# A channel DFT split into even and odd channels, with its sums spread over the product that follows

## The chip, the cores and the metric

The kernel runs on one core of a Trainium2 chip. The metric is the time of one execution in microseconds (us) on the device. Engines are named as in the profile: PE is TensorE's matrix multiply, PEld its weight load, DVE is VectorE, ACT is ScalarE, POOL is GpSimd, SP is SyncE, which here only issues transfers.

## What is computed

Rows of `x` (2048 tokens by 640 channels) are normalized; the result is the sum of `x`, a Fourier transform over channels and tokens of which the real part is kept, and a two-layer product over tokens.

```python
xn = layernorm(x)                                   # (1, 2048, 640)
a = einsum("bsd,ed->bse", xn, dft_hid_re)           # DFT over channels
b = einsum("bsd,ed->bse", xn, dft_hid_im)
y = einsum("ts,bse->bte", dft_seq_re, a) - einsum("ts,bse->bte", dft_seq_im, b)
u = gelu(einsum("bsd,sf->bdf", xn, w1) + b1)        # F = 1728
v = einsum("bdf,fs->bds", u, w2) + b2
out = x + y + v.transpose(0, 2, 1)
```

The kernel has a second way for DFT matrices without the symmetries that it uses; checks of those matrices, which run beside the products, decide at the end whether it is taken. It is not taken here.

## The kernel before

**Stages on TensorE, one after the other.** The first product (`up`, with `w1`); the token DFT (`seq_order`, from L619); the channel DFT (`hid_step`, L736); the second product (`down_step`, L837, with `w2`); then the last row tile is stored. Every float32 matmul is made of three (`three`, L135 to L140): an operand is cut into a high and a low part (`high` on ScalarE L130, `low` on VectorE L133), and high x high, high x low and low x high are accumulated in one bank of PSUM. There are eight banks, taken in turn by `bank()`.

**The channel DFT.** The token DFT leaves blocks T0 to T4 of folded channels: cosine rows of even channels (T0) and odd ones (T1), sine rows (T3, T4), and T2, which mixes what is left of both. The weights of a matmul are 128 tokens of such a block, the moving operand is a piece of the channel matrix with EW = 162 columns for one half of the outputs. Since output 320 - e differs from output e only in the sign of the odd channels, one piece serves both halves. Before, `hid_high` and `hid_low` (L681 to L697) lay each piece twice, the second time with the sign of the odd channels, and `hid_products` (L725) makes three products of 2 x 162 = 324 columns into one bank: T2, the even block, the odd block. The two halves of the bank then hold both halves of the outputs. `part` 0 is cosine, 1 is sine.

A step is one `products(s)` (L741): two groups (`part` 0 and 1), one bank each, for 128 tokens. `hid_step(n, odd, i)` has two steps, s = 0 and 1, and four banks; n runs over `order` (L807): (odd, i) = (1,0), (1,1), (0,0), (0,1). At n = N_MID a fifth bank takes two rows for the middle tokens, with weights of two columns (`t_mid_cut`). When both steps of an n are done, ScalarE copies two of the four banks (`copies`, L753) and VectorE makes sums and differences with the other two (`sums`, L758: four operations of 324); a row of outputs is joined by `whole_rows` (L712: four operations of 159 to 161) and stored to `y_dram`, plain by SP or mirrored by POOL's indirect transfer (`scatter`, L719); ScalarE turns each row round for the mirrored tokens (`read_back`, L775), and that is stored too. So an n makes four pieces of 128 x 640.

**The second product.** 16 row tiles of 128 tokens, each of four steps (i = 0 to 3): 24, 24, 24 and 10 matmuls of 320 columns, 82 in all. The first two tiles go by turns, so that all steps with i = 0 come first. A step's weights, a piece of `w2`, are cut two steps ahead (AHEAD = 2), into three buffers (`cut0` to `cut2`). For tile t, `rest_load` (L872) brings the rows of `y_dram` and of `x`, `rest_sum` (L877) adds them, `down_read` (L880) adds the two banks and `b2`, `store` (L890) writes the tile out.

**What sets the order.** A loop over all steps (L1259 to L1273) writes the instructions out: for step i first what stands in `loads` (SP), then the high part of step i + 2's piece on ScalarE, `reads` (in the token DFT behind the high part, elsewhere ahead), `middle`, the low part on VectorE, `measures`, `behind`, and last the matmuls of step i. `at(i, f)` puts f into such a list. Every engine runs its instructions in this order, and a waiting instruction holds those behind it on its engine; SP too, so a store that waits for its tile holds the loads behind it. s_hid and s_down are the first steps of the channel DFT and of the second product. A step of the second product is counted from s_down in what follows. The checks' 48 loads (`late`, from L1151, 40 by SP and 8 in two parts by POOL) are spread evenly from step `begin` to `n_steps - 9`, each compared five steps after its load.

Of the kernel before, what the change touches and what calls it, by code (L numbers as in the profile page):

```python
# [16 lines left out]
P = 128  # L17
# [32 lines left out]
def fnet_plus_mixer(  # L50
# [630 lines left out]
    def hid_high(q):  # L681
        if not hid_cut:
            hid_cut.append(keep.tile([P, 2, 4, 2, EW], R32, name="hid_main", tag="zt"))
            hid_cut.append(keep.tile([P, 2, 4, EW], R32, name="hid_mix", tag="ck0"))
        hid_main, hid_mix = hid_cut
        raw, by = hid_place[0], -1.0 if q > 1 else 1.0
        nc.scalar.activation(hid_main[:, 0, q, 0], raw[:, q], AF.Copy, scale=by)
        nc.scalar.activation(hid_mix[:, 0, q], raw[:, 4], AF.Identity, scale=mask[:, q : q + 1])

    def hid_low(q):  # L690
        hid_main, hid_mix = hid_cut
        raw, by = hid_place[0], -1.0 if q > 1 else 1.0
        for to, hi, of, times in (
            (hid_main[:, 1, q, 0], hid_main[:, 0, q, 0], q, by), (hid_mix[:, 1, q], hid_mix[:, 0, q], 4, mask[:, q : q + 1])
        ):
            nc.vector.scalar_tensor_tensor(to, raw[:, of], times, hi.bitcast(F32), op0=ALU.mult, op1=ALU.subtract)
        nc.scalar.activation(hid_main[:, :, q, 1], hid_main[:, :, q, 0].bitcast(F32), AF.Copy, scale=-1.0 if q % 2 else 1.0)  # L697
# [4 lines left out]
    def y_place(n):  # L702

        if n not in y_tiles:
            if n % 6 < 2:
                t = keep.tile([P, 2, 2 * D + 1], F32, name=f"y{n}", tag="n3")
                y_tiles[n - n % 2], y_tiles[n - n % 2 + 1] = t[:, 0], t[:, 1]
            else:
                y_tiles[n] = keep.tile([P, 2 * D + 1], F32, name=f"y{n}", tag=f"h{n - 2}")
        return y_tiles[n][:, : D + 1], y_tiles[n][:, D + 1 :]  # L710

    def whole_rows(y, a, b, e=EW):  # L712
        v = nc.vector
        v.tensor_add(y[:, : e4 + 1], a[:, : e4 + 1], b[:, : e4 + 1])
# [21 lines left out]
    def hid_step(n, odd, i):  # L736
# [16 lines left out]
        def copies():  # L753
            held.append(keep.tile([P, 4, 2 * EW], F32, name=f"sums{n}", tag=f"n{1 + n % 2}"))
# [29 lines left out]

        def read_mid():
            a, y = mid_bank[0], keep.tile([P, D], F32, name="y_mid", tag="ck1")[0:2]
            for to, of in (
                (y[:, : e4 + 1], a[:, : e4 + 1]), (y[:, 2 * e4 - 1 : e4 : -1], a[:, EW + 1 : EW + e4]),
                (y[:, 2 * e4 : 3 * e4 + 1], a[:, EW : EW + e4 + 1]), (y[:, D - 1 : 3 * e4 : -1], a[:, 1:e4]),
            ):  # L790
                nc.scalar.activation(to, of, AF.Copy)
# [6 lines left out]
        at(step + 2, copies, when=reads)  # L798
        at(step + 2, sums, when=reads)
        at(step + 2, read(0), when=reads)  # L800
        at(step + 3, read(1), when=reads)
        at(step + 3, read_back(0))
        at(step + 4, read_back(1))
        if n == N_MID:
            at(step + 2, read_mid, when=reads)

    order = [(odd, i) for odd in (1, 0) for i in range(NJ)]  # L807
# [6 lines left out]

    def h_high(i):
# [594 lines left out]
```

## Time and profile before

| | |
|---|---|
| time, median of 3 runs | 442.91 us (442.82 to 443.01) |
| profiled execution | 442.86 us, of which 441.1 is the span between its first and last instruction |
| mean granted clock of TensorE | 0.996 |
| channel DFT, first to last matmul start | 219.83 to 242.32 us |
| second product, first to last matmul start | 242.47 to 434.51 us |
| bytes moved | 105.69 MB |

A time in a row of the timeline is counted from the span's start. In the rows of groups, "x32 | 9.9, 310 | 0.0" is the count, the time in which the group was busy, the mean ns of one, and the idle time ahead. In the rows of waits stand who waited for what, the total in us, the count and the longest. In the rows of windows stand the stretch, its length, each engine's busy time (with the count of instructions), the clock, the busy share of the 16 DMA engines, and GB/s. Transfers of the second product, as the page lists them:

```profile
check<-in_dft_seq SPq DMA_DIRECT2D x58, 512.0 KB
...
w_raw<-in_w SPq DMA_DIRECT2D x16, 512.0 KB
w_raw<-in_w SPq DMA_DIRECT2D x16, 384.0 KB
rest<-y SPq DMA_DIRECT2D x16, 320.0 KB
rest<-in_x SPq DMA_DIRECT2D x16, 320.0 KB
out<-rest SPq DMA_DIRECT2D x15, 320.0 KB
```

### The profile page before, as it was taken

What the parts mean: (1) busy time and instruction counts of PE and PEld (TensorE: products, weight loads), DVE (VectorE), ACT (ScalarE), POOL (GpSimd) and SP (SyncE); (2) the same over time, 40 slices, a digit from 0 to 9 for tenths busy, and PEclk for the clock granted to TensorE, in tenths of its full rate; (3) what the DMA queues carried; (4) which work ended last, traced back from release to release, by engine and by line L of the source; (5) the groups of instructions that cost most, each with busy time, mean ns of one, the idle gap of its engine ahead of it and who ended that gap; (6) DMA issues with size and microseconds to landing.
All of it is one profiled execution on the core that took longest, in us unless ns stands there. A gap on an engine that the chain in (4) does not pass through costs nothing.

```text
span 441.1 us, 8064 instructions
## 1 busy us (share of the span) xinstructions
PE 433.1 (98%) x2963; PEld 427.5 (97%) x2963; DVE 320.4 (73%) x662; ACT 248.5 (56%) x477; POOL 76.7 (17%) x120
## 2 busy tenths in 40 slices
PE   8999999999999999999999999999999999999994
PEld 4999999999999999999999999999999999999993
DVE  6976644776967778777888659677877768688771
ACT  6866673676555655467755535536555455546540
POOL 2055511032220001100023320111302304101000
PEclk9999999999999999999999999999999999999998
DMA  8882508698884760413314999999998998979301
GB/s 291 303 293 83 178 2 292 217 336 291 259 296 161 237 193 25 121 49 97 121 59 192 317 409 403 395 364 357 334 375 309 330 381 292 395 265 347 143 31 39
DMA packets 48176, 105.69 MB, mean 240 GB/s; under 512 B 5732, under 2 KB 6644, under 8 KB 48128
## 3 DMA queue, kind: packets, MB, share of 16 engines
q1 hardware_dynamic: 44816, 93.50, 60.2%
q0 software_dynamic: 3168, 11.42, 7.3%
q8 instruction: 25, 0.41, 0.4%
q14 instruction: 23, 0.19, 0.1%
q10 hardware_dynamic: 144, 0.16, 0.1%
HBM read 94.58 MB, written 10.49 MB: 238 GB/s over the span
## 4 chain that ended last, share of the span: by engine, by line
PE 93%; DVE 3%; DMA 1%; ACT 1%; issue 0%; SPq 0%; DVEq 0%
PE psum L138 26%; PE psum L139 26%; PE psum L140 26%; PE psum L293 9%; PE psum L283 2%; PE psum L863 2%; DMA w_raw<-in_w 1%; DVE early L133 1%; DVE st L200 1%; DVE x L133 1%; ACT early L130 0%; DVE zt L247 0%; DVE r L230 0%; ACT zt L245 0%; DVE again L231 0%
## 5 line engine op out<-in xcount | busy, mean ns | idle before, releaser
L133 DVE TENSOR_TENSOR piece<-w_raw,piece 128x512 fp32r<-128x512 f32 (+2 forms) x128 | 76.4, 598 | 78.3 <-ACT piece L130 69.5
L138 PE MATMUL psum<-h_cut,piece 128*128 128x320 f32 x416 | 128.6, 309 | 0.0
L139 PE MATMUL psum<-h_cut,piece 128*128 128x320 f32 x416 | 128.4, 309 | 0.0
L140 PE MATMUL psum<-h_cut,piece 128*128 128x320 f32 x416 | 128.4, 309 | 0.0
L130 ACT ACTIVATE piece<-w_raw 128x512 fp32r<-128x512 f32 (+2 forms) x112 | 67.0, 600 | 108.5 <-PE psum L140 78.7
L138 PE MATMUL psum<-x,piece 128*128 128x320 f32 x288 | 89.0, 309 | 0.0
L140 PE MATMUL psum<-x,piece 128*128 128x320 f32 x288 | 88.9, 309 | 0.0
L139 PE MATMUL psum<-x,piece 128*128 128x320 f32 x288 | 88.8, 308 | 0.0
L985 ACT ACTIVATE check<-check 128x1024 f32<-128x1024 f32 (+2 forms) x66 | 65.1, 987 | 28.0 <-DVE check L968 11.4
L140 PEld LDWEIGHTS psum<-h_cut,piece 128*128 128x128 f32 x416 | 78.1, 188 | 0.0
L138 PEld LDWEIGHTS psum<-h_cut,piece 128*128 128x128 f32 x416 | 78.1, 188 | 0.0
L139 PEld LDWEIGHTS psum<-h_cut,piece 128*128 128x128 f32 x416 | 78.1, 188 | 0.0
L293 PE MATMUL psum<-x,early 128*128 128x320 f32 x384 | 57.6, 310 | 0.9 <-DVE early L133 0.3
L293 PEld LDWEIGHTS psum<-x,early 128*128 128x128 f32 x384 | 56.3, 188 | 2.1 <-ACT early L130 1.2
L140 PEld LDWEIGHTS psum<-x,piece 128*128 128x128 f32 x288 | 54.1, 188 | 0.0
L138 PEld LDWEIGHTS psum<-x,piece 128*128 128x128 f32 x288 | 54.1, 188 | 0.0
L139 PEld LDWEIGHTS psum<-x,piece 128*128 128x128 f32 x288 | 54.1, 188 | 0.0
L948 POOL DMA_INDIRECT check<-in_dft_seq,from_seq x16 | 19.5, 1221 | 115.7 <-ACT check L985 113.2
L133 DVE TENSOR_TENSOR x<-zt,x 128x640 fp32r<-128x640 f32 x16 | 13.1, 818 | 14.6 <-ACT x L130 14.6
L721 POOL DMA_INDIRECT y<-y,to_mirror x8 | 10.4, 1303 | 57.3 <-DVE y L717 52.7
L883 DVE SCALAR_TENSOR_TENSOR rest<-psum,b_sb,rest 128x320 f32<-128x320 f32 x32 | 16.1, 543 | 1.0 <-PE psum L863 1.0
L966 DVE TENSOR_TENSOR check<-check,check 128x512 f32<-128x512 f32 x24 | 15.4, 685 | 0.0
(215 smaller groups left out, 615.7 us busy)
## 6 DMA issues: line engine op xcount, KB each, us to landing
check<-in_dft_seq SPq DMA_DIRECT2D x58, 512.0 KB
w_raw<-in_w SPq DMA_DIRECT2D x56, 256.0 KB
w_raw<-in_w SPq DMA_DIRECT2D x16, 512.0 KB
w_raw<-in_w SPq DMA_DIRECT2D x16, 384.0 KB
rest<-y SPq DMA_DIRECT2D x16, 320.0 KB
rest<-in_x SPq DMA_DIRECT2D x16, 320.0 KB
out<-rest SPq DMA_DIRECT2D x15, 320.0 KB
ck<-in_dft_seq SPq DMA_DIRECT2D x6, 512.0 KB
```

The costliest lines, as they stand in the source:

```text
L130: nc.scalar.activation(hi, src, AF.Copy)
L133: nc.vector.tensor_sub(lo, src, hi.bitcast(F32))
L138: nc.tensor.matmul(bank, wh, mh, start=first, stop=False, skip_group_check=True)
L139: nc.tensor.matmul(bank, wh, ml, start=False, stop=False, skip_group_check=True)
L140: nc.tensor.matmul(bank, wl, mh, start=False, stop=last, skip_group_check=True)
L283: nc.tensor.matmul(to[half][:, :H2], w[0][:, c], m[i], start=k == to[2] and i == 0, stop=k == to[3] and i == 1, skip_group_check=True,)
L293: nc.tensor.matmul(up_banks[f][half][:, :H2], w_cut[f, k // G][part == 2][:, c], n[:, part == 1, k % 2, half * H2 : (half + 1) * H2], star ...
L721: nc.gpsimd.indirect_dma_start(to, bass.IndirectOffsetOnAxis(ap=to_mirror[:, j : j + 1], axis=0), y, None,)
L883: nc.vector.scalar_tensor_tensor(rest[t][:, 1, cols], down_banks[t][half][:, :H2], b2_sb[:, t : t + 1], rest[t][:, 0, cols], op0=ALU.add, ...
L948: nc.gpsimd.indirect_dma_start(to[:, c * CH : (c + 1) * CH], None, dft_seq.rearrange("c k p t -> (c k p) t"), bass.IndirectOffsetOnAxis(ap ...
L966: (v.tensor_add if odd != (i == 4 and m) else v.tensor_sub)(x1, x0, x1)
L985: nc.scalar.activation(v, v, AF.Square, accum_out=off[:, n : n + 1])
```

## The change

**Products.** The piece of the channel matrix is laid once, without signs. A group multiplies the even block into the first 162 columns of its bank, the odd block into the other 162, and T2 into all 324, with rows of T2's piece masked by parity so that even channels reach the first half alone and odd ones the second. The halves of a bank then hold even and odd channels.

**Sums.** VectorE makes the outputs' halves from them: `by_channels`, per n four operations of 324 elements in SBUF. `whole_rows` does two operations of 320 and 322 in place of four of about 160. The middle rows are copied by ScalarE (`mid_copy`), summed by GpSimd and turned by ScalarE (`read_mid`).

**Order.** n now runs over (1,0), (0,0), (1,1), (0,1); the middle rows belong to n = 1. Sums, channels and rows of each n get steps of their own in `behind`, the later of them in the second product: n = 1's rows at steps 0 and 1, n = 3's sums at step 4, n = 2's channels at 6 and rows at 8 and 9, n = 3's channels at 9 and rows at 14 and 15. The row tiles of the second product go in `down_order`: 0, 1, 6, 7, 8, 9, 14, 15, then 2 to 5 and 10 to 13, so that the first eight need only n = 0 and 1. p is a tile's place in that order. `rest` has three buffers rather than four, the cut hidden values other tiles, and the checks begin at step 6 rather than 1.

```diff
 def hid_high(q):
-        nc.scalar.activation(hid_main[:, 0, q, 0], raw[:, q], AF.Copy, scale=by)
+        nc.scalar.activation(hid_main[:, 0, q], raw[:, q], AF.Copy, scale=by)
 def hid_low(q):
...
-        nc.scalar.activation(hid_main[:, :, q, 1], hid_main[:, :, q, 0].bitcast(F32), AF.Copy, scale=-1.0 if q % 2 else 1.0)
-    def whole_rows(y, a, b, e=EW):
-        v = nc.vector
-        v.tensor_add(y[:, : e4 + 1], a[:, : e4 + 1], b[:, : e4 + 1])
-        v.tensor_sub(y[:, e4 + 1 : 2 * e4], a[:, e + e4 - 1 : e : -1], b[:, e + e4 - 1 : e : -1])
-        v.tensor_add(y[:, 2 * e4 : 3 * e4 + 1], a[:, e : e + e4 + 1], b[:, e : e + e4 + 1])
-        v.tensor_sub(y[:, D : 3 * e4 : -1], a[:, :e4], b[:, :e4])
+    def whole_rows(y, a, b):
+        back = y[:, D:e4:-1].rearrange("p (h e) -> p h e", h=3)[:, ::2]
+        nc.vector.tensor_sub(back, a[:, :, :e4], b[:, :, :e4])
+        to = y[:, :D].rearrange("p (h e) -> p h e", h=2)
+        nc.vector.tensor_add(to[:, :, : e4 + 1], a[:, :, : e4 + 1], b[:, :, : e4 + 1])
-    def hid_products(to, w, part, all_blocks=True):
+    def hid_products(to, w, part):
         hid_main, hid_mix = hid_cut
-        mix, both = hid_mix[:, :, 2 * part : 2 * part + 2], hid_main[:, :, 2 * part : 2 * part + 2]
-        for block, m in (
-            (T2, mix.rearrange("p h q e -> p h (q e)")), ((T0, T3)[part], both[:, :, 0].rearrange("p h s e -> p h (s e)")),
-            ((T1, T4)[part], both[:, :, 1].rearrange("p h s e -> p h (s e)")),
-        ):
-            three(to, w(block), [m[:, j] for j in range(2)], block == T2, block == (T1, T4)[part])
+        for h, block in enumerate(((T0, T1), (T3, T4))[part]):
+            three(to[:, h * EW : (h + 1) * EW], w(block), [hid_main[:, j, 2 * part + h] for j in range(2)], h == 0, False)
+        m = hid_mix[:, :, 2 * part : 2 * part + 2].rearrange("p h q e -> p h (q e)")
+        three(to, w(T2), [m[:, j] for j in range(2)], False, True)
+        def by_channels():
+            a = held[0].rearrange("p s (h e) -> p (s h) e", h=2)
+            for part in range(2):
+                even, o = (a[:, 4 * part + h : 4 * part + 4 : 2] for h in range(2))
+                nc.vector.tensor_add(a[:, 8 + 2 * part : 10 + 2 * part], even, o)
+                nc.vector.tensor_sub(o, even, o)
+        def mid_copy():
+            mid = keep.tile([P, D + 2 * EW], F32, name="y_mid", tag="ck1")[0:2]
+            nc.scalar.activation(mid[:, D:], mid_bank[0], AF.Copy)
+            mid_bank.append(mid)
         def read_mid():
...
+            nc.gpsimd.tensor_add(y[:, : e4 + 1], even, o)
+            nc.gpsimd.tensor_sub(y[:, 2 * e4 : 3 * e4 + 1], even, o)
-        at(step + 2, copies, when=reads)
-        at(step + 2, sums, when=reads)
-        at(step + 2, read(0), when=reads)
-        at(step + 3, read(1), when=reads)
-        at(step + 3, read_back(0))
-        at(step + 4, read_back(1))
+        at(step + 2 + 2 * (n == 3), copies, when=reads)
+        after = ((2, 3, 4, 5), (2, 5, 6, 7), (2, 10, 12, 13), (6, 11, 16, 17))[n]
+        at(step + after[0], sums, when=behind)
+        at(step + after[1], by_channels, when=behind)
+        for s in range(2):
+            at(step + after[2 + s], read(s), when=behind)
+            at(step + after[2 + s] + 1, read_back(s))
-    order = [(odd, i) for odd in (1, 0) for i in range(NJ)]
+    order = [(odd, i) for i in range(NJ) for odd in (1, 0)]
+    down_order = [t for last in range(2) for t in range(NS) if (t + 2) % 8 // 4 == last]
-        rest[t] = keep.tile([P, 2, D], F32, name=f"rest{t}", tag=f"h{t % 4}")
+        rest[t] = keep.tile([P, 2, D], F32, name=f"rest{t}", tag=f"h{down_order.index(t) % 3}")
-            at(s_down + 4 * t - (t > 0), rest_load, t, when=loads)
-            at(s_down + 4 * t + 2 + 3 * (t == 0), rest_sum, t)
+            when = -6 if p < 2 else p - 1 + 4 * i if p < 4 else 4 * p - 6
+            at(s_down + when, w2_load, t, i, when=loads)
+            at(s_down + (5 + 2 * p if p < 2 else 4 * p + 1), rest_load, t, when=loads)
+            at(s_down + (8 + p if p < 2 else 4 * p + 3), rest_sum, t)
-            nc.vector.tensor_mul(mask[:, i + 1 : i + 2], mask[:, i : i + 1], parity[:, 2:3])
+            nc.vector.tensor_mul(mask[:, i + 1 : i + 2], mask[:, i : i + 1], parity[:, 1:2])
+            nc.vector.tensor_mul(mask[:, i : i + 1], mask[:, i : i + 1], parity[:, 0:1])
-    begin, last = s_down + 1, n_steps - 9
+    begin, last = s_down + 6, n_steps - 9
```

On TensorE, the first group of the channel DFT, before: `hid_mix` is T2's piece, `hid_main` the others', t0 and t1 are the high and low parts of the weights.

```order
L138 MATMUL psum5_103<-hid_mix_2210,t0_2413 128x324
L139 MATMUL psum5_103<-hid_mix_2210,t0_2413 128x324
L140 MATMUL psum5_103<-hid_mix_2210,t1_2414 128x324
L138 MATMUL psum5_103<-hid_main_2209,t0_2413 128x324
L139 MATMUL psum5_103<-hid_main_2209,t0_2413 128x324
L140 MATMUL psum5_103<-hid_main_2209,t1_2414 128x324
```

The same group now, behind a first `hid_main` triple of the same rows as the one shown:

```order
L138 MATMUL psum5_103<-hid_main_2211,t0_2411 128x162
L139 MATMUL psum5_103<-hid_main_2211,t0_2411 128x162
L140 MATMUL psum5_103<-hid_main_2211,t1_2412 128x162
L138 MATMUL psum5_103<-hid_mix_2212,t0_2411 128x324
L139 MATMUL psum5_103<-hid_mix_2212,t0_2411 128x324
L140 MATMUL psum5_103<-hid_mix_2212,t1_2412 128x324
```

T2 has moved behind the others, and `hid_main` has half the columns; the count of matmuls is the same, nine to a group.

On VectorE, steps 3 to 5 of the second product before (`piece` is a low part of `w2`, `rest` the sum of rows):

```order
L133 TENSOR_TENSOR piece_2957<-w_raw_134,piece_2957 128x512
L133 TENSOR_TENSOR h_cut6_2959<-h6_2363,h_cut6_2959 128x1280
L133 TENSOR_TENSOR piece_2989<-w_raw_134,piece_2989 128x256
L133 TENSOR_TENSOR piece_2989<-w_raw_134,piece_2989 64x128
L878 TENSOR_TENSOR rest0_2834<-rest0_2834 128x640
L133 TENSOR_TENSOR piece_3025<-w_raw_134,piece_3025 128x256
```

And now, steps 6 to 9:

```order
L768 TENSOR_TENSOR sums2_2749<-sums2_2749 128x324
L769 TENSOR_TENSOR sums2_2749<-sums2_2749 128x2x162
L133 TENSOR_TENSOR piece_3032<-w_raw_134,piece_3032 128x512
L904 TENSOR_TENSOR rest0_2973<-rest0_2973 128x640
L133 TENSOR_TENSOR piece_3046<-w_raw_134,piece_3046 128x512
L714 TENSOR_TENSOR y4_3050<-sums2_2749 128x2x160
L716 TENSOR_TENSOR y4_3050<-sums2_2749 128x2x161
L904 TENSOR_TENSOR rest1_3028<-rest1_3028 128x640
L133 TENSOR_TENSOR piece_3083<-w_raw_134,piece_3083 128x256
```

Channels and rows of n = 2 now stand between pieces, and the sum of the first tile's rest rows stands at step 8, behind them.

On SP, the transfers from one store to the next, before (`check` is a load of the checks, `in_w` is `w2`, `y2_94` and `y3_95` are the third and fourth quarter of `y_dram`):

```order
L892 DMA out<-rest6_3555 128x640
L833 DMA w_raw_134<-in_w2 128x1024
L833 DMA w_raw_134<-in_w2 128x768
L954 DMA check1_2987<-in_dft_seq 128x2x512
L874 DMA rest8_3797<-y2_94 128x640
L875 DMA rest8_3797<-in_x 128x640
L954 DMA check0_2880<-in_dft_seq 128x2x512
L892 DMA out<-rest7_3676 128x640
```

And now, at a like place (tile 14 is the seventh in the new order):

```order
L918 DMA out<-rest8_3344 128x640
L859 DMA w_raw_134<-in_w2 128x1024
L859 DMA w_raw_134<-in_w2 128x768
L980 DMA check1_3081<-in_dft_seq 128x2x512
L980 DMA check0_3006<-in_dft_seq 128x2x512
L900 DMA rest14_3592<-y3_95 128x640
L901 DMA rest14_3592<-in_x 128x640
L980 DMA check0_3006<-in_dft_seq 128x2x512
L918 DMA out<-rest9_3467 128x640
```

The rest load has moved towards the store behind it, past a load of the checks.

More of the change, by code (lines that the diff above doesn't have):

```diff
@@ L682, in hid_high @@
         if not hid_cut:
-            hid_cut.append(keep.tile([P, 2, 4, 2, EW], R32, name="hid_main", tag="zt"))
+            hid_cut.append(keep.tile([P, 2, 4, EW], R32, name="hid_main", tag="zt"))
             hid_cut.append(keep.tile([P, 2, 4, EW], R32, name="hid_mix", tag="ck0"))
@@ L753, in copies @@
         def copies():
-            held.append(keep.tile([P, 4, 2 * EW], F32, name=f"sums{n}", tag=f"n{1 + n % 2}"))
+            held.append(keep.tile([P, 6, 2 * EW], F32, name=f"sums{n}", tag=f"n{1 + n % 2}"))
             for part in range(2):
@@ L783, in read_back @@
             return run
+        def mid_copy():
+            mid = keep.tile([P, D + 2 * EW], F32, name="y_mid", tag="ck1")[0:2]
+            nc.scalar.activation(mid[:, D:], mid_bank[0], AF.Copy)
+            mid_bank.append(mid)
         def read_mid():
[L786 to L791, printed above, removed]
+            y, (even, o) = mid_bank[1][:, :D], (mid_bank[1][:, D + h * EW :][:, : e4 + 1] for h in range(2))
+            nc.gpsimd.tensor_add(y[:, : e4 + 1], even, o)
+            nc.gpsimd.tensor_sub(y[:, 2 * e4 : 3 * e4 + 1], even, o)
+            for h in range(2):
+                begin = 2 * e4 * h
+                nc.scalar.activation(y[:, D - 1 - begin : 3 * e4 - begin : -1], y[:, begin + 1 : begin + e4], AF.Copy)
             for s in range(2):
@@ L852, in products @@
             blocks = range(4 * i, min(4 * i + 4, NFB))
-            by_half = t == NS - 1 and last
+            by_half = t == down_order[-1] and last
             pairs = [(f, half) for f in blocks for half in range(2)]
             for f, half in sorted(pairs, key=lambda pair: pair[1]) if by_half else pairs:
-                c, h = slice((f - 4 * i) * P, (f - 4 * i + 1) * P), n_tiles["h", f // 2]
+                c, h = slice((f - 4 * i) * P, (f - 4 * i + 1) * P), h_cut[f // 2]
                 cols = slice(half * H2, (half + 1) * H2)
-                to, m = down_banks[t][half][:, :H2], [h[:, which, f % 2, cols] for which in range(2)]
+                to, m = down_banks[t][half][:, :H2], [a[:, f % 2, cols] for a in h]
                 if f < NF:
@@ L886, in down_read @@
             )
[L887 removed]
+            if t == down_order[-1]:
                 (nc.sync, nc.scalar)[half].dma_start(out_rows[t][:, cols], rest[t][:, 1, cols])
     def store(t):
[L891 removed]
+        if t != down_order[-1]:
             nc.sync.dma_start(out_rows[t], rest[t][:, 1])
[L895 to L904 removed]
+    turns = [(p, i) for i in range(4) for p in range(2)] + [(p, i) for p in range(2, NS) for i in range(4)]
+    for n, (p, i) in enumerate(turns):
+        t = down_order[p]
+        if i < 2:
+            when = -6 if p < 2 else p - 1 + 4 * i if p < 4 else 4 * p - 6
+            at(s_down + when, w2_load, t, i, when=loads)
+        if i == 0:
+            at(s_down + (5 + 2 * p if p < 2 else 4 * p + 1), rest_load, t, when=loads)
+            at(s_down + (8 + p if p < 2 else 4 * p + 3), rest_sum, t)
+            done = s_down + (10 + p if p < 2 else 4 * p + 4)
+            at(done, down_read, t, when=reads)
+            at(min(done + 1, s_down + 4 * NS), store, t)
         down_step(t, i, i == 0, i == 3)
[L906 to L908 removed]
     n_steps = len(steps)
@@ L1182, in fnet_plus_mixer @@
     at(n_first + 35, lambda: nc.vector.memset(t_mid, 0.0))
-    for i, when in enumerate((s_seq + 3, s_seq + 6, s_hid + 1, s_hid + 3, s_hid + 5, s_down + 1, s_down + 3)):
+    for i, when in enumerate((s_seq + 3, s_seq + 6, s_hid + 1, s_hid + 3, s_down, s_down + 1, s_down + 3)):
         at(when, h_high, i)
```

51 lines of the change are left out of this document (24 added, 27 removed).

## The prediction

> **What bounds the kernel now.** I read the page first: its first rows, the slices, and the chain of work that ended last.
>
> ```profile
> span 441.1 us, 8064 instructions
> ...
> PE 433.1 (98%) x2963; PEld 427.5 (97%) x2963; DVE 320.4 (73%) x662; ACT 248.5 (56%) x477; POOL 76.7 (17%) x120
> ...
> PE   8999999999999999999999999999999999999994
> ...
> PE 93%; DVE 3%; DMA 1%; ACT 1%; issue 0%; SPq 0%; DVEq 0%
> ```
>
> TensorE is busy in every slice but the first and last, and it makes 93% of the chain. So matmul time that goes comes off the end, unless a wait takes its place. The busy figure can't price a matmul, since neighbours overlap. I price by the distance between starts, from the timeline of TensorE and of its weight loads.
>
> ```profile
> 216.72 0.28 PE L139 MATMUL psum<-piece,f 128*128 128x258 f32 x1
> ...
> 219.35 0.28 PE L140 MATMUL psum<-piece,f 128*128 128x258 f32 x1
> ...
> 219.83 0.32 PE L138 MATMUL psum<-hid_mix,t 128*128 128x324 f32 x1
> ...
> 222.50 0.31 PE L138 MATMUL psum<-hid_mix,t 128*128 128x324 f32 x1
> ...
> 242.47 0.31 PE L138 MATMUL psum<-h_cut,piece 128*128 128x320 f32 x1
> ```
>
> From 219.83 to 222.50 stand 18 matmuls of 324 columns: **148.3 ns** each. From 216.72 to 219.35 stand 22 of 258 columns: 119.5 ns each. So a column costs (148.3 - 119.5)/66 = 0.436 ns, and 162 columns alone would ask 119.5 - 96 x 0.436 = 77.6 ns. The channel stage lasts from 219.83 to 242.47, 22.64 us.
>
> Every matmul also loads weights of 128 columns. What that costs is hidden behind 324 columns, but there is one place with very short matmuls.
>
> ```profile
> 72.06 1.01 PEld L421 LDWEIGHTS psum<-norm_cut,places_of 128*128 128x128 f32 x8
> 72.98 0.19 PEld L138 LDWEIGHTS psum<-x,piece 128*128 128x128 f32 x1
> 73.09 0.19 PEld L139 LDWEIGHTS psum<-x,piece 128*128 128x128 f32 x1
> ...
> 72.20 0.96 PE L421 MATMUL psum<-norm_cut,places_of 128*128 128x32 f32 x8
> ```
>
> Eight matmuls of 32 columns start at 72.20. A load starts when the matmul ahead of it starts to stream, so the eighth streams at 72.98: seven distances in 0.78 us, **111 ns** each, and 0.11 us again to 73.09. That is a floor under any matmul here which loads 128 columns.
>
> **The change: TensorE.** A group (one `hid_products`) is nine matmuls of 324 columns before. After, six have 162 columns and three keep 324. There are 8 steps x 2 parts = 16 groups, and one more for the middle rows, as the counts by shape show.
>
> ```profile
> L138 PE MATMUL psum<-hid_main,t 128*128 128x324 f32 x32 | 9.9, 310 | 0.0
> ...
> L138 PE MATMUL psum<-hid_mix,t 128*128 128x324 f32 x16 | 5.0, 310 | 0.0
> ...
> L138 PE MATMUL psum<-hid_main,t_mid_cut 128*2 128x324 f32 x2 | 0.6, 311 | 0.0
> ...
> L138 PEld LDWEIGHTS psum<-hid_mix,t_mid_cut 128*2 128x2 f32 x1 | 0.1, 83 | 0.0
> ...
> L421 PEld LDWEIGHTS psum<-norm_cut,places_of 128*128 128x128 f32 x8 | 1.0, 191 | 0.0
> ```
>
> Line 138 issues one of three terms, so 96 + 6 matmuls shrink. The 96 go from 148.3 to 111 ns, not to 77.6: 96 x 37.3 = 3.58 us. The six of the middle group load two columns; that load takes 83 ns against 191, 108 less, so the floor is nearly gone: 6 x (148.3 - 77.6) = 0.42 us. Sum **-4.0 us**. Bounds: no matmul faster than its columns, 102 x 70.7 = -7.2 us; none gained, 0. I take the floor, because the eight matmuls are the same kind of load.
>
> A rule that speaks against the change: the Trainium skill, page "TensorE: Matmul & The Clock Gate", section "The mechanism", says that a weight load runs beside a matmul only where their row groups differ. By it, load and stream would add up for our full-height weights: 111 + 77.6 against 148.3, so 96 x 40.3 = +3.9 us in the place of -3.6. The trace disagrees: 258 columns with a load each stand 119.5 ns apart, where load and stream would ask 111 + 112.
>
> **Does anything feed TensorE too late in the shorter stage?** A group now takes 6 x 111 + 3 x 148.3 = 1.11 us, an n (four groups) 4.45, the middle group 0.91. From 219.83, n=0 ends at 224.3, n=1 (with the middle group) at 229.6, n=2 at 234.1, n=3 at 238.5. VectorE's prices:
>
> ```profile
> 222.99 0.17 DVE L133 TENSOR_TENSOR t_mid_cut<-t_mid,t_mid_cut 128x6 fp32r<-128x6 f32 x1 [0.31 <-ACT t_mid_cut L130]
> ...
> 236.04 1.49 DVE L133 TENSOR_TENSOR h_cut<-h,h_cut 128x1280 fp32r<-128x1280 f32 x1 [1.03 <-ACT h_cut L130]
> ...
> 237.45 0.49 DVE L760 TENSOR_TENSOR sums<-psum,sums 128x324 f32<-128x324 f32 x1
> ...
> 239.31 0.32 DVE L714 TENSOR_TENSOR y<-sums 128x161 f32<-128x161 f32 x1
> ...
> 240.25 0.68 DVE L133 TENSOR_TENSOR piece<-w_raw,piece 128x512 fp32r<-128x512 f32 x1
> ...
> 240.86 0.32 DVE L714 TENSOR_TENSOR y<-sums 128x161 f32<-128x161 f32 x1
> ```
>
> By starts: `h_cut` 1.4, four `sums` 1.9, four row operations 0.94, a piece 0.6 us. Not in the trace: an addition of 324 elements, SBUF to SBUF. Four rows of 160 cost 0.94 and 512 cost 0.61, so 324 lie between 0.24 and 0.61; by the straight line 0.41, and with the gap between two that depend, about 0.45. So `by_channels` (four) costs 1.8 us, and the new `whole_rows` (two of 320) 0.9, what the four short ones cost. Net +1.8 us x 4 = 7.2 us on VectorE, none of it on TensorE's path if three deadlines hold:
>
> - The middle weights `t_mid_cut` end at 223.16; the middle products, now before n=1 rather than n=2, start at 224.3. Margin 1.1 us.
> - VectorE then does `h_cut` 2, sums, channels and half the rows of n=0, `h_cut` 3 (1.4 + 1.9 + 1.8 + 1.4 + 0.9, to 230.6) and the sums of n=1, to 232.5. n=3 takes those banks at 234.1. Margin 1.6 us.
> - The sums of n=2 follow its end at 234.1 by a copy on ScalarE (0.45) and 1.9 us; the first row tile takes the banks at 238.5. Margin about 2 us.
>
> So nothing here, but the margins are short. Were they missed by 2 us or more, 2 to 4 us would come back.
>
> **The change in the second product.** Between two pieces VectorE now has up to 2.7 us of new work (rows of n=2 and channels of n=3, step 9). What covers it:
>
> ```profile
> ACT piece L130 <- PE psum L140: 60.8, 32, 3.1
> ...
> 264.39 0.69 DVE L133 TENSOR_TENSOR piece<-w_raw,piece 128x512 fp32r<-128x512 f32 x1 [1.82 <-ACT piece L130]
> ...
> 266.46 0.31 PE L138 MATMUL psum<-h_cut,piece 128*128 128x320 f32 x1
> ...
> 265.92 0.69 DVE L133 TENSOR_TENSOR piece<-w_raw,piece 128x512 fp32r<-128x512 f32 x1
> ```
>
> ScalarE waits for TensorE to free a piece's buffer 32 times: cutting runs as far ahead as three buffers let it. The tightest piece, behind two short steps, ends at 265.08, 1.4 us before its matmul at 266.46. The next ends at 266.61, 3.4 us before it is wanted (24 matmuls, 3.5 us, after 266.46). 2.7 us fit in 3.4 where each step brings 3.5: cost 0; without that cover 2.7 us, once. The sums of n=3 (1.9 us, step 4) and the channels of n=2 (1.8, step 6) fit likewise.
>
> The **transfers** are the open term. SP now stops at `y` stores in the second product, and the checks start at step 6 instead of 1, so 48 loads come in 49 steps instead of 54.
>
> ```profile
> core 0: us, PE busy (x) PEld busy (x) DVE busy (x) ACT busy (x) POOL busy (x), PEclk, DMA share, GB/s
> 242.40:266.40 24.00, 24.00 (x166) 24.00 (x165) 14.51 (x29) 10.47 (x18) 7.21 (x7) 1.00 1.00 366
> 266.40:302.40 36.00, 36.00 (x248) 36.00 (x247) 28.71 (x48) 18.60 (x37) 5.21 (x5) 1.00 1.01 381
> 302.40:362.40 60.00, 60.00 (x412) 60.00 (x411) 45.41 (x76) 32.37 (x68) 10.09 (x8) 1.00 0.96 346
> ...
> 250.00:254.00 4.00, 4.00 (x29) 4.00 (x28) 0.97 (x3) 1.77 (x4) 1.04 (x1) 1.00 1.00 309
> ...
> DMA packets 6964, 16.09 MB, mean 402 GB/s; under 512 B 625, under 2 KB 625, under 8 KB 6960
> ...
> ACT piece L130 <- DMA w_raw<-in_w: 1.0, 1, 1.0
> ...
> DVE rest L878 <- DMA rest<-in_x: 0.3, 1, 0.3
> ```
>
> The windows show the 16 DMA engines full (share 1.00) from 242 to 302; the row on packets is that of 254 to 294. Yet ScalarE waited for weights once, 1.0 us, VectorE for rest rows 0.3 us, and TensorE for nothing. Four steps take 12.0 us (82 matmuls). In them go 3.6 checks of 0.52 MB before and 3.9 after, weights 0.92 MB, rest rows 0.66, one store 0.33 and check rows of the channel matrix 0.33: 4.1 MB before, 4.3 after. From step 6 on, the four tiles of 48 us also carry the eight `y` pieces of n=2 and 3: 4 x 4.28 + 2.6 = 19.7 MB. At 402 GB/s that is 1 us late, at 381 3.7, at 346/0.96 = 360 6.7. Pieces bear 3.4 us of it. So the cost lies between 0 and 3.3 us; at 381, the row nearest to that stretch and the middle of the three, it is **+0.3 us**, which I take.
>
> The Trainium skill, page "DMA: Bandwidth & Descriptors", section "Where 436 GB/s comes from", puts the HBM side at about 358 GB/s per core; by that estimate the transfers would be 7 us late. The 402 GB/s over 40 us disagree.
>
> ScalarE loses four sign copies and one of four short copies of the middle rows; GpSimd gets two additions on two rows. Neither holds TensorE: 0. The last tile ends as before (halves, two stores): 0.
>
> **Sum.** The profiled execution took 442.86 us (span 441.1, 1.8 around it), the median of the runs is 442.91, so they may be read as one. 442.86 - 4.0 + 0.3 = **439.2 us**.
>
> **Rivals.** *The transfers fall behind for part of the way.* For it: 309 GB/s at a full share from 250 to 254, when `y` pieces moved. Against: 402 just after. Stalls of 0.6 to 3.3 us: 439.5 to 442.2.
>
> *Slower: VectorE stuck at the sum of rest rows.* A rest load now stands two steps later in SP's order (step 4p + 1 rather than 4t - 1), its sum only one step later (4p + 3 rather than 4t + 2), and VectorE works in order, so the next piece waits behind that sum. It decides from a rate under 350 GB/s over that stretch: 19.7 MB are then 8.3 us late, 4.9 beyond what pieces bear, which is 4.0 + 0.9. At 345 it is 9.1 late: 442.86 - 4.0 + 5.7 = 444.6. For it: the row with 309. Against: 366, 381 and 346 as means, the last with TensorE dense throughout.
>
> *The stage's margins break*, since VectorE (19.3 of 22.6 us busy there by the window below) has less time: a bank or the middle weights late by 3 to 4 us, 442 to 443.
>
> ```profile
> 219.80:242.40 22.60, 22.60 (x155) 22.02 (x154) 19.32 (x54) 13.72 (x31) 5.82 (x5) 1.00 0.31 119
> ```
>
> *The floor isn't there* at 162 columns: -7.2 us, 435.9. Against it is the row of eight. *Loads aren't hidden*, each short matmul 111 + 77.6 = 189 ns: 442.86 + 3.9 - 0.4 = 446.4. Against it are the 119.5 ns. This is what the rule of the Trainium skill named above would make of the kernel. *The change doesn't do what it says*: the rows of the program show 162 columns, so no.
>
> **How the numbers follow.** Forecast (438.5 to 439.5) 0.58; transfers behind (to 442.2) 0.21; VectorE stuck 0.08; margins broken 0.07; no floor 0.05; loads not hidden 0.01. About 0.2%, 0.9 us, is what a measurement of this kernel can tell from no change: faster means under 442.0, slower over 443.8. Faster: 0.58 + 0.21 + 0.05 = 0.84; same: 0.07; slower: 0.08 + 0.01 = 0.09. The forecast and the transfers hold 0.79; so the range is 438.5 to 442.2: without the floor's absence, with both bounds of the transfers.
>
> **What would show it.** In the channel stage: starts of 162-column matmuls 111 ns apart, 148 for 324, the stage 18.7 us long from 219.8. 78 apart would refute the floor, 189 the hiding. A gap ahead of the middle group, of n=3 or of the first row tile would refute a margin. In the second product: no matmul gap over 0.2 us; if there are any, near the third to eighth tile, behind a piece that waited behind a sum of rest rows or for weights, with the DMA share at 1.00. I am wrong if the stage is shorter and the end is not.

## The result, and the profile after

| | before | changed |
|---|---|---|
| time, median | 442.91 us (five runs, 442.64 to 443.03) | 445.24 us (five runs; four of them 444.65 to 446.36) |
| ratio | | 1.0054, interval 1.004 to 1.0068 |
| profiled execution | 442.86 us | 446.36 us |
| channel DFT, first matmul start to that of the second product | 22.64 us | 18.72 us |
| second product, first to last matmul start | 192.04 us | 199.63 us |

The changed kernel is 0.5% slower; the forecast was 439.2 us. The fifth execution of the changed kernel took 1700.16 us for a cause that wasn't looked into, so it counts in the median alone, and the ratio and the range are those of the other four, whose own median is 444.97 us.

The page of the changed kernel, with the span, the slices of TensorE and its clock, and the chain that ended last:

```profile
span 444.6 us, 8069 instructions
...
PE   9999999999999999999999999995999999999994
...
PEclk9999999999999999999999999997999999999999
...
PE 88%; DMA 6%; DVE 4%; ACT 1%; issue 0%; SPq 0%; DVEq 0%; ACTq 0%
```

One slice of forty, the 28th, has a hole in TensorE and a low clock, and transfers (6%) and VectorE (4%) are in the chain, where TensorE had 93% before. Everything else is the stage getting shorter. First that stage, in TensorE's timeline:

```profile
220.29 0.24 PE L138 MATMUL psum<-hid_main,t 128*128 128x162 f32 x1
220.37 0.27 PE L139 MATMUL psum<-hid_main,t 128*128 128x162 f32 x1
...
220.93 0.35 PE L138 MATMUL psum<-hid_mix,t 128*128 128x324 f32 x1
...
221.41 0.23 PE L138 MATMUL psum<-hid_main,t 128*128 128x162 f32 x1
...
224.75 0.24 PE L138 MATMUL psum<-hid_main,t_mid_cut 128*2 128x162 f32 x1
...
225.21 0.31 PE L138 MATMUL psum<-hid_mix,t_mid_cut 128*2 128x324 f32 x1
...
239.01 0.31 PE L138 MATMUL psum<-h_cut,piece 128*128 128x320 f32 x1
```

From 220.37 to 220.93 stand five distances of 112 ns, and a group takes 221.41 - 220.29 = 1.12 us. With weights of two columns, six matmuls of the same 162 columns (224.75 to 225.21) take 77 ns each. From 220.29 to 239.01 no start is more than 0.19 us behind the one ahead: none of the three margins broke.

Now the hole. TensorE's, then VectorE's timeline, with the idle time ahead and its releaser in brackets:

```profile
302.66 0.31 PE L139 MATMUL psum<-h_cut,piece 128*128 128x320 f32 x1
307.59 0.63 PE L140 MATMUL psum<-h_cut,piece 128*128 128x320 f32 x1 [4.63 <-DVE piece L133]
308.03 0.47 PE L138 MATMUL psum<-h_cut,piece 128*128 128x320 f32 x1
```

```profile
301.01 0.15 DVE L1005 COPY check<-check 128x1 f32<-128x1 f32 x1
306.11 0.82 DVE L904 TENSOR_TENSOR rest<-rest 128x640 f32<-128x640 f32 x1 [4.95 <-DMA rest<-in_x]
306.86 0.68 DVE L133 TENSOR_TENSOR piece<-w_raw,piece 128x512 fp32r<-128x512 f32 x1
```

VectorE stands 4.95 us at the sum of rest rows (L904) at place p = 4, step 19, and the low part of the piece (L133) that step 21 needs stands behind it. TensorE's starts are 4.94 us apart in the place of 0.15, so the wait reaches TensorE almost whole. The rows were late because SP reached their loads late, as its timeline and its waits show:

```profile
277.13 0.34 SPq L918 DMA_DIRECT2D out<-rest  x1
284.42 0.33 SPq L900 DMA_DIRECT2D rest<-y  x1
284.80 0.42 SPq L901 DMA_DIRECT2D rest<-in_x  x1
...
288.21 1.12 SPq L778 DMA_DIRECT2D y<-y  x1
...
292.02 0.34 SPq L786 DMA_DIRECT2D y<-y  x1
292.41 0.54 SPq L900 DMA_DIRECT2D rest<-y  x1
293.97 0.33 SPq L901 DMA_DIRECT2D rest<-in_x  x1
```

```profile
SPq L900 <- DMA out<-rest: 6.9, 1, 6.9
```

At 277.13 SP issues a store and then stands 6.9 us before the rest load at p = 3: with three buffers that load takes the tile of p = 0, whose store hasn't landed. All later transfers stand behind it. From 284.5 to 294.4 SP waits 2.7 us in all, and it has two `y` stores, checks, a store and weights to issue before the next rest load. The load at p = 4 goes out at 292.41 and 293.97, in step 17, which begins at 239.01 + 4 x 12.0 + 3.5 = 290.5: SP is 1.9 to 3.5 us behind TensorE. The kernel before issued its rest load for the fifth tile in step 15 at 284.64 and 285.47:

```profile
284.64 0.77 SPq L874 DMA_DIRECT2D rest<-y  x1
285.47 0.42 SPq L875 DMA_DIRECT2D rest<-in_x  x1
```

Step 15 begins there at 242.47 + 48.0 - 1.5 = 289.0, so SP was 3.5 to 4.4 us ahead. Next the windows, with clock, share of the transfers and GB/s at a row's end: first that of the kernel before over 60 us, then those of the changed kernel.

```profile
242.40:302.40 60.00, 60.00 (x412) 60.00 (x411) 43.22 (x76) 29.07 (x55) 12.42 (x12) 1.00 1.01 375
```

```profile
242.40:302.40 60.00, 60.00 (x413) 60.00 (x412) 44.15 (x78) 28.46 (x54) 12.65 (x11) 1.00 0.88 311
...
254.00:262.00 8.00, 8.00 (x56) 8.00 (x55) 4.13 (x10) 1.25 (x3) 0.00 (x0) 1.00 0.52 168
...
278.00:286.00 8.00, 8.00 (x57) 8.00 (x56) 5.01 (x10) 3.32 (x7) 0.00 (x0) 1.00 0.96 365
...
302.40:307.60 5.20, 0.57 (x5) 0.31 (x4) 1.49 (x3) 0.53 (x2) 0.00 (x0) 0.89 1.04 414
307.60:313.40 5.80, 5.80 (x22) 5.80 (x23) 4.58 (x8) 1.15 (x2) 1.39 (x2) 0.51 1.04 398
```

The share of 0.88 doesn't come from SP's stop: the idle time of the transfers lies mostly ahead of 262 us, where the checks have hardly begun, and in the stop itself the engines were nearly full (0.96). From 262.0 to 302.4 the share is 0.97, with 354 GB/s. The last row is the second part of the loss. For 5.8 us behind the hole the granted clock is 0.51, and matmuls start 0.27 us apart (308.03 and after) in the place of 0.146.

**The account** (starts of matmuls): stage 18.72 - 22.64 = -3.9; hole 4.94 - 0.15 = +4.8; the 21 slow distances behind it +2.7; 0.1 elsewhere. The second product is 7.6 us longer, the stage began 0.5 us later, the tail after the last matmul is 0.6 shorter: +3.5 us, as the spans (441.1 and 444.6) have it. The profiled execution is the slowest of the four; the medians differ by 2.3 us, and the others weren't traced.

### The profile page after: what moved, and what is told of

It reads as the page before. It is cut to its first block, busy times and chain, and to the rows that moved or that the text cites. A ratio compares the mean times of both kernels' runs of the same rounds, so it can differ in the third digit from the quotient of the medians.

```text
span 444.6 us, 8069 instructions
## 1 busy us (share of the span) xinstructions
PE 432.9 (97%) x2963; PEld 426.9 (96%) x2963; DVE 326.1 (73%) x664; ACT 246.7 (55%) x472; POOL 77.7 (17%) x122
## 4 chain that ended last, share of the span: by engine, by line
PE 88%; DMA 6%; DVE 4%; ACT 1%; issue 0%; SPq 0%; DVEq 0%; ACTq 0%
PE psum L138 25%; PE psum L140 25%; PE psum L139 25%; PE psum L293 9%; DMA w_raw<-in_w 3%; DMA rest<-in_x 3%; PE psum L283 2%; PE psum L889 2%; DVE early L133 1%; DVE st L200 1%; DVE x L133 1%; ACT early L130 0%; DVE zt L247 0%; DVE r L230 0%; ACT zt L245 0%
## 5 line engine op out<-in xcount | busy, mean ns | idle before, releaser
L133 DVE TENSOR_TENSOR piece<-w_raw,piece 128x512 fp32r<-128x512 f32 (+2 forms) x128 | 76.4, 597 | 73.4 <-ACT piece L130 70.2
L140 PE MATMUL psum<-h_cut,piece 128*128 128x320 f32 x256 | 80.2, 313 | 4.6 <-DVE piece L133 4.6
L138 PE MATMUL psum<-h_cut,piece 128*128 128x320 f32 x256 | 80.2, 313 | 0.0
L139 PE MATMUL psum<-h_cut,piece 128*128 128x320 f32 x256 | 80.0, 313 | 0.0
L140 PEld LDWEIGHTS psum<-h_cut,piece 128*128 128x128 f32 x256 | 49.2, 192 | 4.9 <-DVE piece L133 4.9
L138 PE MATMUL psum<-h_high,piece 128*128 128x320 f32 x160 | 49.7, 310 | 0.0
L140 PE MATMUL psum<-h_high,piece 128*128 128x320 f32 x160 | 49.5, 309 | 0.0
L139 PE MATMUL psum<-h_low,piece 128*128 128x320 f32 x160 | 49.4, 309 | 0.0
L138 PEld LDWEIGHTS psum<-h_cut,piece 128*128 128x128 f32 x256 | 49.1, 192 | 0.0
L139 PEld LDWEIGHTS psum<-h_cut,piece 128*128 128x128 f32 x256 | 49.1, 192 | 0.0
L138 PEld LDWEIGHTS psum<-h_high,piece 128*128 128x128 f32 x160 | 30.1, 188 | 0.0
```

Of the source, the lines that this page charges most:

```text
L133: nc.vector.tensor_sub(lo, src, hi.bitcast(F32))
L138: nc.tensor.matmul(bank, wh, mh, start=first, stop=False, skip_group_check=True)
L139: nc.tensor.matmul(bank, wh, ml, start=False, stop=False, skip_group_check=True)
L140: nc.tensor.matmul(bank, wl, mh, start=False, stop=last, skip_group_check=True)
```

## The experiments

My theory: the loss is one load that SP reaches too late, with VectorE stuck at its sum, and a clock that falls in the hole. Rivals: the volume of transfers (whichever comes first, something is late), a clock that falls by itself, and a gap that the other order of tiles or VectorE's bursts make. The kernel before was timed beside each of them, with medians of 443.03 to 443.18 us. "Gap" is the largest distance of two starts of the second product in the profiled execution, "slow" the starts at half clock behind it.

| run | median us | ratio, interval | gap us | slow |
|---|---|---|---|---|
| load of rest rows two steps earlier | 441.14 | 0.9954, 0.9941 to 0.9966 | 2.28 | none |
| sum behind the piece | 441.21 | 0.997, 0.9953 to 0.9988 | 2.41 | none |
| checks from step 1 | 444.39 | 1.0036, 1.002 to 1.0053 | 1.83, 2.73 | 11 |
| before, checks from step 6 | 442.72 | 0.9991, 0.9982 to 1.0 | none | none |
| four buffers | 441.05 | 0.9961, 0.9947 to 0.9976 | 2.04 | none |
| four buffers, earlier load | **438.76** | 0.9901, 0.9885 to 0.9917 | none | none |
| the same, sum behind | 439.29 | 0.9914, 0.9899 to 0.9928 | none | none |
| before, the change's rest schedule | 442.64 | 0.9994, 0.9985 to 1.0003 | none | none |
| the same, checks from step 6 | 442.74 | 0.9989, 0.998 to 0.9998 | none | none |
| last rows of y later | 441.3 | 0.997, 0.9952 to 0.9989 | 1.31 | none |
| before, twelve additions | 449.95 | 1.0156, 1.0139 to 1.0174 | 5.87 | 14 |
| before, seven additions | 444.3 | 1.0025, 1.0015 to 1.0034 | 1.56 | none |

### The load two steps earlier

```diff
-            at(s_down + (5 + 2 * p if p < 2 else 4 * p + 1), rest_load, t, when=loads)
+            at(s_down + ((5, 7, 9, 13)[p] if p < 4 else 4 * p - 1), rest_load, t, when=loads)
```

> The changed kernel with one edit: the rest rows of a row tile at place p are loaded at step 4p - 1 again, as before the change, in the place of 4p + 1 (places 0 to 3 stay, since their buffers come free no earlier). The order alone (one load that SP reaches too late, and VectorE stuck at its sum): the wait of 4.95 us at the sum of rest rows and TensorE's gap of 4.9 us go, the granted clock stays at 1.0, and 7.5 us come back: 438.9 us, within 438.3 and 440. The volume (too many transfers behind the checks' late start, whichever comes first): the rest rows come in time and the weights two steps later, so that TensorE waits 2 to 5 us for a piece: 441 to 445. The clock by itself (a drop that the gap didn't cause): the gap goes, 2.6 us of slow matmuls stay: 441.5.

441.14 us, with a gap of 2.28 us at the same place: a miss for the order alone, and by its number within what I gave the volume. But the piece that TensorE waited for was not short of weights, as the volume would have it: it stood behind the same sum, at which VectorE waited 2.50 us for the rest rows. The slow clock went with the smaller gap, so it isn't a thing by itself. The gap stayed because SP was still stopped, as this run's waits show:

```profile
SPq L900 <- DMA out<-rest: 7.3, 1, 7.3
```

Behind that stop the second half of the load at p = 4 went out at 290.44 rather than 293.97, 3.5 us sooner and no more, though two steps lie between (5.0 us, one of them the short one).

### The sum behind the piece

```diff
-            at(s_down + (8 + p if p < 2 else 4 * p + 3), rest_sum, t)
+            at(s_down + (8 + p if p < 2 else 4 * p + 3), rest_sum, t, when=behind)
```

> The changed kernel with one edit: the sum of rest rows stays in its step, but behind the step's piece on VectorE, so that this piece no longer waits for the rows. The order alone: one more step's work is ahead of the late rows, 2.9 us; of the gap of 4.9 us some 2 us are left, and a gap this short brings little or no drop of the clock: 440.5 to 442. The volume: the piece then waits for its weights in the same way, 443 to 445. If VectorE's queue had nothing to do with it: 445.2, as the changed kernel.

441.21 us, as the theory had it. The rows landed as late as ever (VectorE's sum at 305.98), but the gap came one step later and was 2.41 us. So VectorE's order passes the lateness on to TensorE. Ten of twelve executions took 440.7 to 442.3 us with a mean clock of 0.995 to 0.998, two took 443.5 and 445.3 with 0.992 and 0.990: these two weren't traced, but by their clock this gap is near the size at which the clock falls.

### Checks from step 1

```diff
-    begin, last = s_down + 6, n_steps - 9
+    begin, last = s_down + 1, n_steps - 9
```

> The changed kernel with one edit: the checks of the input begin at step 1 of the second product, as before the change, in the place of step 6; loads and sums of rest rows stay where the change put them. The volume: 48 check loads are spread over 54 steps again, the idle stretch of the DMA engines from 254 to 262 us is used, and the stall goes: 438.9 to 440. The order alone: the load of rest rows still stands two steps later, and SP still stops at the stores of y; the transfers ahead of it are some 0.5 to 1 MB less, 1.2 to 2.5 us, so the wait of 4.95 us shrinks to 2.5 to 4: 440.5 to 444.

444.39 us, just above the upper end that the theory gave, and far from the volume's 438.9 to 440. The old gap was still 2.73 us, with a slow clock, and there was a new one of 1.83 us at 274.91. The new gap brought TensorE 1.7 us later to the old place, which is why the old one is shorter: the sum of rest rows began at 305.63, only 0.5 us sooner than in the changed kernel (306.11), though the transfers now used the stretch from 254 to 262 us (405 GB/s rather than 168). VectorE's timeline of this run ahead of the new gap:

```profile
270.91 0.49 DVE L768 TENSOR_TENSOR sums<-sums 128x324 f32<-128x324 f32 x1
...
272.79 1.41 DVE L994 SCALAR_TENSOR_TENSOR check<-check,parity,check 128x512 f32<-128x512 f32 x2
274.23 0.75 DVE L1001 SCALAR_TENSOR_TENSOR check<-check,parity 128x512 f32<-128x512 f32 x1
...
276.00 0.68 DVE L133 TENSOR_TENSOR piece<-w_raw,piece 128x512 fp32r<-128x512 f32 x1
```

No transfer is waited for there: the channels of an n and a check's compare fill VectorE, and the piece comes late. The bursts do cost something when checks run beside them; the change's later start of the checks keeps them apart.

### The kernel before with checks from step 6

> The kernel before with one edit of the change: the checks begin at step 6 of the second product in the place of step 1. The volume: 48 check loads in 49 steps alone bring the stall, 2 to 7 us: 445 to 450. The order alone: loads and sums of rest rows stand early, so VectorE isn't stuck: 442.9, within 442.5 and 443.8.

The same line in the kernel before, the other way round: 442.72 us, no gap. Its transfers ran at 204 GB/s (share 0.55) from 254 to 262 us, an idle stretch like the changed kernel's, and nothing came of it. With the run above, the late start of the checks is refuted as the cause.

### Four buffers, and both edits together

```diff
-        rest[t] = keep.tile([P, 2, D], F32, name=f"rest{t}", tag=f"h{down_order.index(t) % 3}")
+        rest[t] = keep.tile([P, 2, D], F32, name=f"rest{t}", tag=f"h{(0, 1, 2, 6)[down_order.index(t) % 4]}")
```

> The changed kernel with one edit: rest rows go round in four buffers, as before the change, in the place of three (the fourth is that of the seventh row tile of h, free by then); the places of loads and sums stay. In the changed kernel SP stood 6.9 us at the load of rest rows at place 3, for the landing of the store whose buffer it takes, with all later transfers behind it. SP's stop: without it the transfers of 277 to 284 us go out up to 7 us earlier, the rest rows at place 4 land before their sum, and the gap of 4.9 us with its slow clock goes or falls under 1 us: 439 to 440. The volume: the 16 DMA engines were nearly full in that stop (365 GB/s), so the later loads land no earlier, and the gap stays at 3 to 5 us: 443 to 445.

441.05 us, between the two: SP's timeline in this run, and VectorE's, show what the buffer gave.

```profile
276.96 0.34 SPq L918 DMA_DIRECT2D out<-rest  x1
278.66 0.33 SPq L900 DMA_DIRECT2D rest<-y  x1
...
292.10 0.43 SPq L901 DMA_DIRECT2D rest<-in_x  x1
```

```profile
303.14 0.83 DVE L904 TENSOR_TENSOR rest<-rest 128x640 f32<-128x640 f32 x1 [2.76 <-DMA rest<-in_x]
```

The stop at p = 3 is gone (278.66 rather than 284.42), but its 5.8 us shrink to 1.9 by the load at p = 4, which SP still issues behind the `y` stores and checks. The rows land 3 us sooner, and the wait is 2.76 us.

```diff
-            at(s_down + (5 + 2 * p if p < 2 else 4 * p + 1), rest_load, t, when=loads)
+            at(s_down + (5 + 2 * p if p < 2 else 4 * p - 1), rest_load, t, when=loads)
```

> The changed kernel with two edits: four rest buffers as in the run before, and the load of rest rows at step 4p - 1 from place 2 on, as before the change. SP's stop and the place of the load together: no gap over 0.5 us, 438.9 us, within 438.3 and 439.8. The load's place alone gave 441.1 with a gap of 2.3 us; if the volume were the cause, the gap would stay at about that: 440.5 to 441.5.

With both, 438.76 us: 1.0% below the kernel before, and the fastest of all. The page, and VectorE's timeline at the place of the hole:

```profile
span 436.8 us, 8076 instructions
...
PE   8999999999999999999999999999999999999994
```

```profile
298.71 0.83 DVE L904 TENSOR_TENSOR rest<-rest 128x640 f32<-128x640 f32 x1
```

The sum waits for nothing, and the second product takes 192.15 us, 0.1 more than before the change. The volume itself is refuted here: the same 105.7 MB go, with the same idle stretch (176 GB/s from 254 to 262 us), and no gap is left.

> The changed kernel with three edits: four rest buffers, the load at step 4p - 1, and the sum of rest rows behind the step's piece on VectorE. If the run with two edits has no gap left, this is the same: 438.9, within 0.4 us of it. If a gap is left there, this takes another 0.5 to 2 us off it. VectorE's order as a cause of its own in other places: it could cost where the result of a tile is read a step later; at most 0.5 us.

With the sum behind the piece as well, 439.29 us: nothing left to win, as expected.

### What of the change makes the load late

The schedule of rest rows was put into the kernel before:

```diff
-        rest[t] = keep.tile([P, 2, D], F32, name=f"rest{t}", tag=f"h{t % 4}")
+        rest[t] = keep.tile([P, 2, D], F32, name=f"rest{t}", tag=f"h{t % 3}")
-            at(s_down + 4 * t - (t > 0), rest_load, t, when=loads)
-            at(s_down + 4 * t + 2 + 3 * (t == 0), rest_sum, t)
+            at(s_down + (5 + 2 * t if t < 2 else 4 * t + 1), rest_load, t, when=loads)
+            at(s_down + (8 + t if t < 2 else 4 * t + 3), rest_sum, t)
-            at(len(steps), down_read, t, when=reads)
-            at(min(len(steps) + 1, NS * 4 + s_down), store, t)
+            done = s_down + (10 + t if t < 2 else 4 * t + 4)
+            at(done, down_read, t, when=reads)
+            at(min(done + 1, NS * 4 + s_down), store, t)
```

> The kernel before with the whole schedule of rest rows of the change (three buffers, loads at step 4p + 1, sums at 4p + 3, and results of the first two tiles read and stored at steps 10 to 12), but the old order of row tiles, the old rows of y and checks from step 1. If this schedule is enough by itself: SP stops at the load at place 3, and TensorE gets a gap of 1 to 5 us: 444 to 448. If it needs the burst of y stores and gathers that the change put into these steps: no gap, 442.9, within 442.4 and 443.5. I lean to the second, as y moves here before step 7.

> The run before this one (the kernel before with the change's schedule of rest rows) and checks from step 6 as well. If the schedule and the squeezed checks make the stall together: a gap of 1 to 5 us, 444 to 448. If the y stores and gathers in the second product are needed: 442.9, within 442.4 and 443.5.

442.64 and 442.74 us, no gap in either, though SP's waits in the first show the same stop:

```profile
SPq L874 <- DMA out<-rest: 5.3, 1, 5.3
```

So the late load and the missing buffer aren't enough. In the first of these runs the load for the fifth tile went out at 290.36, 3.6 us sooner than in the changed kernel, and TensorE was 3.8 us later, since its second product began at 242.77 rather than 239.01: SP was 3.9 us ahead of step 17 in the place of 3.5 behind. What is missing there is the shorter channel stage, the new order of row tiles, and `y` in the second product, with VectorE's work for it. Of these, `y` was tried: in the changed kernel, its last rows were moved eight steps back:

```diff
-        after = ((2, 3, 4, 5), (2, 5, 6, 7), (2, 10, 12, 13), (6, 11, 16, 17))[n]
+        after = ((2, 3, 4, 5), (2, 5, 6, 7), (2, 10, 12, 13), (6, 11, 24, 25))[n]
```

> The changed kernel with one edit: the last rows of y (n=3: their additions, stores and the gathers behind them) come at steps 22 and 23 of the second product in the place of 14 and 15; the schedule of rest rows is left as the change has it. The kernel before with that schedule had no gap, so the y rows in this stretch should be the missing part: 4 stores and gathers of y less ahead of the rest rows at place 4, some 2.6 MB with what they read, so these rows land before their sum or 1 to 2 us behind it: no gap or one under 2 us at 302 us and no slow clock, 438.9 to 441; if the transfers then pile up 8 steps later, a gap there. If the y rows play no part (the other order of tiles or VectorE's bursts instead): a gap of 4 to 5 us, 444.5 to 446.

441.3 us with a gap of 1.31 us, 0.3 above the range but with the gap and clock that it named. Two of the twelve executions took 444.0 and 444.94 us with a mean clock of 0.994 and 0.989. SP's timeline in this run has the load at p = 4 3.9 us sooner than the changed kernel:

```profile
290.11 0.34 SPq L901 DMA_DIRECT2D rest<-in_x  x1
```

So three things each put the load at p = 4 back: its step, the buffer, and the `y` rows ahead of it. Taking away any one leaves a gap of 1.3 to 2.3 us; the load's step and the buffer together leave none. What the earlier TensorE, the other order of tiles and the rows of n = 2 add was not tried by itself.

### The price of a gap

Additions on VectorE in the kernel before, which write rest rows that are read no more:

```diff
         nc.vector.tensor_add(rest[t][:, 0], rest[t][:, 0], rest[t][:, 1])
+        if t == 8:
+            for _ in range(12):
+                nc.vector.tensor_add(rest[t][:, 1], rest[t][:, 1], rest[t][:, 1])
```

> The kernel before, which has no gap, with twelve additions of 640 elements put on VectorE behind the sum of rest rows of the ninth tile (some 9.8 us; they write rest rows that nobody reads any more), to price a gap of TensorE by itself. Its pieces bear some 3.4 us and VectorE's idle time another 1 to 2: a gap of 4 to 5.5 us. The gap alone: 442.9 + 4 to 5.5 = 447 to 448.5, matmuls at 146 ns behind it. With the clock's drop as in the changed kernel: some 21 matmuls at 267 ns behind the gap, 2.6 us more, 449.5 to 451.

449.95 us. TensorE's timeline in this run:

```profile
350.63 0.31 PE L139 MATMUL psum<-h_cut,piece 128*128 128x320 f32 x1
356.50 0.63 PE L140 MATMUL psum<-h_cut,piece 128*128 128x320 f32 x1 [5.56 <-DVE piece L133]
356.93 0.47 PE L138 MATMUL psum<-h_cut,piece 128*128 128x320 f32 x1
```

The time is within the range for a clock that drops. A gap of 5.87 us, a little longer than expected, then 14 slow starts, the first 0.43 and the others mostly 0.27 us apart (1.8 us more, where 2.6 was expected): the clock falls here too, in a kernel that has nothing of the change.

> The kernel before with seven in the place of twelve additions on VectorE, 4.1 us less: a gap of 1.5 to 2 us. The clock drops only behind a gap over some 2.4 to 2.7 us (so the gaps seen until now): no slow matmuls, 442.9 + 1.8 = 444.7, within 444.2 and 445.2. Any gap of some us lowers the clock: 446 to 447.

With seven additions 444.3 us, within the range. The same view:

```profile
350.83 0.31 PE L139 MATMUL psum<-h_cut,piece 128*128 128x320 f32 x1
352.39 0.41 PE L140 MATMUL psum<-h_cut,piece 128*128 128x320 f32 x1 [1.25 <-DVE piece L133]
352.64 0.31 PE L138 MATMUL psum<-h_cut,piece 128*128 128x320 f32 x1
352.79 0.31 PE L139 MATMUL psum<-h_cut,piece 128*128 128x320 f32 x1
```

One start 0.25 us behind the gap, then 0.15 again: no slow clock. This is why each of the four single edits (load, sum, buffers, `y` rows) wins about 4 us by the medians (4.1 to 5.8 by the profiled executions) though it takes off only 2.5 to 3.6 us of gap: below some 2.5 us the clock's 2.7 us go with it.

## Why the prediction was wrong

- **TensorE, -4.0 us: right.** The stage is 3.9 us shorter, with 112 ns for 162 columns by the floor of the weight load (111 in the forecast) and 77 with two-column weights (77.6). The run with both edits took 438.76 us, where 442.86 - 4.0 gives 438.9.
- **The stage's margins, 0: right.** No gap in the stage.
- **Bursts of VectorE in the second product, 0: right for this kernel.** The run with checks from step 1 showed 1.7 us where the cover was gone.
- **Transfers, +0.3 us with a bound of 3.3: this step failed.** It measured 4.8 us of gap, and its working was wrong in two places. First, it divided bytes by a rate, as if all transfers were late together. What counts is when SP reaches one load, and the step doesn't follow SP there: it doesn't mention the buffer of p = 0, where SP stood 6.9 us, and it gives the two later steps of the load no price. At the 354 GB/s that were moved from 262 to 302.4 us the same division gives 55.6 us, 7.6 late and 4.2 beyond the 3.4, close to the 4.8; but this is no cause, since with four buffers and the earlier load the same bytes went at 381 GB/s over that stretch and nothing was late. Second, "pieces bear 3.4 us" is the cover behind an ordinary step. The sum stands ahead of the piece for the second step after a tile's short last step, where VectorE had just finished a check: a wait of 4.95 us became a gap 4.8 us longer than normal, so the cover was 0.15 us.
- **The clock: put at nothing, without a reason.** In the profiled execution it cost 2.7 us, and 1.5 and 1.8 us behind the two other long gaps. Every gap that I priced (the margins, the transfers up to 3.3 us) was priced without it.
- **The rival "VectorE stuck at the sum of rest rows" came true**, with 0.08. Place and mechanism were right. That its 444.6 us are near the 445.24 is luck: its 5.7 us are a wait alone, where the profiled execution has 4.8 us of gap and 2.7 of slow clock. Its deciding point, a rate under 350 GB/s over that stretch, was the wrong quantity: 354 were measured there, so it would not have decided for what came. It should have been decided by SP's order, where the load stood behind a stop for a buffer and two `y` stores, 1.9 to 3.5 us behind TensorE in the place of 4 us ahead.
- "I am wrong if the stage is shorter and the end is not" is what happened.

Open is how the 12.0 us from issue to landing of that load (7.7 in the median of its line on the page) divide among the transfers ahead of it, and what the 3.9 us by which TensorE comes earlier to the second product took from SP's lead.

## What to carry to other kernels

When a change moves a load later or takes away a buffer, follow the issuing queue itself, instruction by instruction, up to the load: a wait for a buffer or a store ahead of it delays everything behind, whatever the mean bandwidth says. Take the cover of a consumer at the very place where it stands, not the usual one, and price a gap of TensorE of more than 2.5 us with the slow clock behind it (1.5 to 2.7 us here). A change may be right in its main part and lose by a side condition: here one more buffer and two steps turned 0.5% slower into 1.0% faster.

## What the runs showed of the hardware

Here a gap of TensorE lowered its granted clock to about half (0.51 in the changed kernel) from a certain length on. Starts 1.31, 1.56, 1.83, 2.04, 2.28 and 2.41 us apart were followed by matmuls at 146 ns; 2.73, 4.94 and 5.87 us by matmuls at 267 ns, for 3.3, 5.8 and 3.9 us. In these three the time at half clock doesn't grow with the gap. The Trainium skill, page "TensorE: Matmul & The Clock Gate", section "Part 1: The HAM clock gate (the "warmup" mystery)", tells of a free-running monitor that halves the clock after an idle window of about 3.4 us and restores it after a busy one. The halving (267 ns for 146) and the spread of the slow time (3.3 to 5.8 us) agree; but 2.73 us from start to start, 2.42 of them idle by the profile, were enough here, so the figure of 3.4 us isn't a safe bound.
